# Working from PSUM in a spectral front, and a routing laid out without small copies

## The chip, the cores and the metric

One core of one Trainium2 chip runs the whole program in one launch. The metric is device time in microseconds (us). Engines are named as in the profile: PE is TensorE's matmul, PEld its weight load, DVE is VectorE, ACT is ScalarE, POOL is GpSimd, SP issues most of the DMAs.

## The reference, cut to what matters

```python
# front: x is (8, 3072, 256); 24576 tokens in all
X = np.fft.rfft(x, axis=1)                       # Xr, Xi
Yr = Xr @ w_r - Xi @ w_i + b_r
Yi = Xr @ w_i + Xi @ w_r + b_i
Y* = sign(Y*) * max(abs(Y*) - 0.01, 0)           # shrinkage
y  = np.fft.irfft(Y, n=3072, axis=1)             # token rows
# routing: 8 experts, the best one for each token
logits = y @ w_gate;  e = argmax(logits);  gate = softmax(logits)[e]
# experts, each on its own tokens
out[mask] = gate * (relu(y[mask] @ w1[e]) @ w2[e])
# last: two products, multiplied, then w3 and w_out
result = ((out @ W1) * (out @ W2)) @ w3 @ w_out
```

## The kernel before

The program has three parts: the front (transform, linear layer, shrinkage, inverse transform, routing), the experts (windows of 512 or 256 rows of one expert) and a last part of dense products. Every float32 product is made as three fp32r products of a high and a low part (`mm3`, L98); the high part is an ACT copy, the low part a subtraction on DVE or POOL.

The front factors 3072 = 48 x 64 and has three stages that run interleaved. Stage a (`stage_a`, L195) works on 64 tiles t: it loads a piece of x, splits it (`dxh` by ACT, `dxl` by POOL from t = 11 on), transforms over one factor and stores to DRAM. Stage b (`stage_b`, L235) makes 96 steps n, each for a pair of values k of k1. `dft2` (L246) multiplies into a PSUM bank; X gets the high part of it (ACT, L258), the low part (DVE, L259), and, for the second half of the linear layer, the negated first half of both parts (DVE, L262, SBUF to SBUF). X has three buffers and `dft2` runs three k ahead of the linear layer. `linear` (L264) makes 24 matmuls a k pair into a bank `pl`; then DVE adds the bias from `pl` into an SBUF tile s (L283 or L285), clamps s into m (L286) and subtracts m from s (L287), ACT rounds s into sh (L288) and DVE makes the low part sl (L289). `inv1` (L292) consumes sh and sl one step later. Stage c (`stage_c`, L325) works on 64 tiles t: `inv2` (L337) makes the token rows y, `flip` (L344) transposes them through PE, ACT and DVE split them (yh, yl, L351 and L352), `logits` (L355) multiplies by the gate weights. Four tiles t, as four groups g, are accumulated in one PSUM bank, and after the fourth `route` (L398) runs once for their 1536 tokens: 16 times in all.

`route` transposes the logits on DVE (L404), finds the expert by small DVE operations on 128 partitions x 12 x 8 (L415 to L435), counts tokens ahead of each by four doubling steps of an addition and a copy (L430, L431); and `late` (L437), one tile t later, adds a matmul for the rows above, gets the row in `xs`, moves 12 blocks of 32 x 8 into the layout of y by small copies (L452), casts the row numbers (L454), and writes gate and token number behind each row of y (L458, L459). The 16 rows of indices are then scattered by 16 indirect DMAs from POOL (L388), at most six for each tile t in program order.

The queue of each engine is in order. A planner (`schedule_with_timeline_sim=True`) places the instructions on the queues by its own model of costs, from the order of the program, the free buffers and the eight PSUM banks (pool `ps`, one bank a tile). The stages are interleaved in program order by L936 to L954: eight tiles of a and c for 12 steps of b, c lagging 15 steps.

Of the kernel before, what the change touches and what calls it, by code (L numbers as in the profile page):

```python
# [81 lines left out]
def misc_constants():  # L82
    ident = np.eye(128, dtype=np.float32)
    tri = np.zeros((128, 256), np.float32)
    tri[:, :128] = np.triu(np.ones((128, 128)), 1)
    tri[:, 128:] = 1.0
    small = np.zeros((128, 128), np.float32)
    small[:, 0:8] = 8 - np.arange(8)
    small[:, 8:16] = np.arange(8) * CAP
    small[:, 16:18] = np.where(np.arange(128) < 64, 1.0, -1.0)[:, None]  # L90
    small[96, 17] = 1.0
    small[:, 18:26] = np.arange(8)
    small[:, 32:96] = np.arange(64)
    small[:P96, 96:128] = np.arange(S).reshape(P96, 32)
    return [ident, tri, small]


def mm3(nc, out, a, b, first=True, last=True):  # L98
    """out (+)= a.T @ b, a and b as (high, low) parts; the product of the low parts is below float32's last bit."""
    nc.tensor.matmul(out, a[0], b[0], start=first, stop=False)  # L100
    nc.tensor.matmul(out, a[0], b[1], start=False, stop=False)  # L101
    nc.tensor.matmul(out, a[1], b[0], start=False, stop=last)  # L102


class Front:
# [17 lines left out]
    def const(self, pool, name, shape, src=None, fill=True):  # L123
        """A constant as (high, low) parts."""
# [39 lines left out]
    def consts_c(self, pool):  # L164
        nc = self.nc
        self.g2 = self.const(pool, "c_g2", [P96, P96])
        # gate weights, spread so that four quads of tokens land on four groups of partitions
        raw = self.p["s"].tile([128, 512], F32, name="s")
        wg = raw[:, :2 * NE].rearrange("p (c e) -> p c e", c=2)
        nc.sync.dma_start(wg, self.ins["moe_w_gate"].rearrange("(c p) e -> p c e", p=128))  # L170
        self.sg = pool.tile([128, 2, 4, 128], F32R, name="sg")
        nc.gpsimd.memset(self.sg.bitcast(F32), 0.0)
        for g in range(4):
# [3 lines left out]
        raw = self.p["s"].tile([128, 512], F32, name="s")  # L177
# [4 lines left out]
        zero = self.p["s"].tile([128, 2 * D], F32, name="s")  # L182
# [52 lines left out]
    def stage_b(self):  # L235
        """A step for each pair of values of k1, over all batches."""
# [9 lines left out]
        def dft2(n):  # L246
# [13 lines left out]
            if k:  # L260
                # [Q | P] is followed by -Q
                nc.vector.tensor_scalar(X[:, :, :, 128:192], X[:, :, :, 0:64].bitcast(F32), -1.0, None, op0=ALU.mult)  # L262

        def linear(n):  # L264
# [12 lines left out]
            s = self.p["s"].tile([128, 512], F32, name="s")  # L277
# [3 lines left out]
            if i:  # L281
                bias = self.bias[:, D:2 * D].unsqueeze(1).to_broadcast([128, 2, D])
                nc.vector.tensor_tensor(s.rearrange("p (k e) -> p k e", k=2), pl.rearrange("p (k e) -> p k e", k=2), bias, op=ALU.add)  # L283
# [41 lines left out]
    def stage_c(self):  # L325
# [18 lines left out]
        def flip(t):  # L344
            for c in range(2):
# [3 lines left out]
                yh = self.p["yt"].tile([128, 384], F32R, name="yh")  # L349
                yl = self.p["yt"].tile([128, 384], F32R, name="yl")  # L350
                nc.scalar.activation(out=yh, in_=pt[:, :384], func=AF.Copy)  # L351
                nc.vector.tensor_tensor(yl, pt[:, :384], yh.bitcast(F32), op=ALU.subtract)  # L352
                yt[t, c] = yh, yl

        def logits(t):  # L355
            g = t % 4
# [6 lines left out]
            if g == 3:  # L363
# [5 lines left out]
        for t in range(n + 3):  # L369
# [4 lines left out]
            if t < n:  # L374
                inv2(t)
            if 1 <= t < n + 1:
                flip(t - 1)
            late, self.late = self.late, None
            if 2 <= t < n + 2:
                logits(t - 2)  # L380
# [17 lines left out]
    def route(self, b, h, pg, ys):  # L398
        """Expert, gate and row of 1536 tokens: (g, t) x (jj, pb) has p = 32 pb + t, j = 8 g + 4 h + jj."""
        nc, r = self.nc, self.p["r"]  # L400
        V = nc.vector
        NC = 12
        lgt = r.tile([128, 384], F32, name="lgt")
        V.transpose(lgt, pg[:, :384])  # L404
        lg4 = lgt.rearrange("p (k i) -> p k i", i=32)

        def t3(name, dt=F32):
            return r.tile([128, NC, NE], dt, name=name)

        def wide(ap):  # L410
            return ap.to_broadcast([128, NC, NE])

        lg, sh, v, oh, ex = t3("lg"), t3("shf"), t3("vv"), t3("oh", BF16), t3("ex")
        m1 = [r.tile([128, NC, 1], F32, name=f"m1{i}") for i in range(4)]
# [3 lines left out]
        io = wide(self.small[:, 0:8].unsqueeze(1))  # L418
# [4 lines left out]
        pair = r.tile([128, NC, 2], F32, name="pair")  # L423
        # how many tokens of the same expert come before: in the columns before, and in the rows above
        W = NC * NE
        cur = oh.rearrange("p k e -> p (k e)")
        for i, d in enumerate((1, 2, 4, 8)):
            nxt = r.tile([128, W], BF16, name=f"pre{i}")
            n = d * NE
            V.tensor_tensor(nxt[:, n:], cur[:, n:], cur[:, :W - n], op=ALU.add)  # L430
            V.tensor_copy(nxt[:, :n], cur[:, :n])  # L431
            cur = nxt
        V.tensor_reduce(out=m1[2], in_=ex, axis=AX.X, op=ALU.add)
        V.tensor_scalar(m1[3], m1[2], 1e-9, None, op0=ALU.add)
        V.reciprocal(pair[:, :, 1:2], m1[3])  # L435

        def late():  # L437
            pr = self.ps.tile([128, 512], F32, name="ps")
            nc.tensor.matmul(pr[:, :W], self.tri[:, 0:128], oh.rearrange("p k e -> p (k e)"), start=True, stop=False)
            nc.tensor.matmul(pr[:, NE:W], self.tri[:, 128:256], cur[:, :W - NE], start=False, stop=True)  # L440
            nc.tensor.matmul(pr[:, 256:256 + NE], self.tri[:, 128:256], cur[:, W - NE:W], start=True, stop=True)
            rk, rs = t3("rk"), t3("rs")
            V.tensor_tensor(rk, pr[:, :W].rearrange("p (k e) -> p k e", e=NE), wide(self.cnt.unsqueeze(1)), op=ALU.add)
            V.tensor_tensor(rs, rk, oh, op=ALU.mult)
            V.tensor_reduce(out=pair[:, :, 0:1], in_=rs, axis=AX.X, op=ALU.add)
            V.tensor_tensor(self.cnt, self.cnt, pr[:, 256:256 + NE], op=ALU.add)
            # (g, t) x (jj, pb) -> (pb, t) x (g, jj)
            p2 = r.tile([P96, 4, 4, 2], F32, name="pair2")
            pv = pair.rearrange("p (k b) w -> p k b w", b=3)
            for g in range(4):  # L450
                for pb in range(3):
                    V.tensor_copy(p2[32 * pb:32 * pb + 32, g], pv[32 * g:32 * g + 32, :, pb, :])  # L452
            it = r.tile([P96, 16], I32, name="it", bufs=2)
            V.tensor_copy(it, p2[:, :, :, 0].rearrange("p g j -> p (g j)"))  # L454
            for g in range(4):
                # a row of xs: the row of y, its gate, its number
                j0 = 96 + 8 * g + 4 * h
                V.tensor_copy(ys[g][:, :, D], p2[:, g, :, 1])  # L458
                V.tensor_scalar(ys[g][:, :, D + 1], self.small[:P96, j0:j0 + 4], float(S * b), None, op0=ALU.add)  # L459
# [12 lines left out]
# Order of the last steps: b and c are stages of the front part, d is a step of the experts;  # L472
# the second string starts once the pools of the first stages are free.
# [3 lines left out]
class Experts:  # L477
    """The experts, over windows of rows of one expert each: 41 of 512 rows, and 21 of 256 rows.

    Whatever the counts, at least 41 full windows exist, and what they leave (3584 rows, in 8 parts) fits  # L480
    into 21 windows of 256: a part of n * 256 + r rows takes n + 1, of which the last one overlaps. Five
    batches and a half hold 26 full windows. The results are columns of dout, without gaps: first the experts of 256
    rows and more, then the others, in the order of their windows, as each of these spills over what the next
    one writes; the windows that are left over write behind the last column.
    """
# [13 lines left out]
    # small arithmetic on the counts  # L499
# [24 lines left out]
    def running(self, a, p=1):  # L524
        """Sums over the experts up to each, with it and without it."""
# [11 lines left out]
    def pick(self, w, incl, excl):  # L537
        """[1, w, 8]: whether window number w is one of the expert's."""
# [6 lines left out]
    def total(self, m, v, sh, out):  # L545
        """out = sum over the experts of m * v."""
# [6 lines left out]
    def full(self, w0, w1):  # L553
        """Windows w0 to w1 of 512 rows: the counts so far hold that many."""
# [26 lines left out]
    def rest(self):  # L581
        """The windows of 256 rows, and where every window's results go."""
# [18 lines left out]
        # the first column of every expert, against its first row of xs  # L601
# [425 lines left out]
```

## Time and profile before

| quantity | value |
|---|---|
| device time, three runs | 3786.15, 3791.05, 3792.51 us (median 3791.05) |
| span of the profiled execution | 3780.3 us (its time outside the span is not listed) |
| mean granted TensorE clock | 0.974 of full |
| busy over the span: PE, DVE, ACT, POOL | 95%, 53%, 45%, 36% |
| instructions: PE, DVE, ACT, POOL | 20592, 3595, 3073, 947 |

The share of busy time is a mean over parts with different limits. The front takes about the first 980 us; the experts come in from about 850 us; the last part begins at about 2100 us, and from there PE is busy without a gap. A matmul's duration in the trace is a latency: matmuls overlap, so the spacing of two starts is what one costs, and a PE that is busy all the time may still be short of its rate.

### The profile page before, as it was taken

The numbers are of one execution on the slowest core, as the hardware profiler recorded it, in microseconds if no ns is written. First come the engines' busy times: TensorE is split into PE (matmuls) and PEld (weight loads), VectorE is DVE, ScalarE is ACT, GpSimd is POOL, SyncE is SP. The second block draws the span as 40 slices with busy tenths as digits, with TensorE's granted clock in tenths as the row PEclk, the third lists the DMA queues.
The fourth block names the chain that finished last, engine by engine and source line by source line (L and its number), as shares of the span: only waits on it lengthen the run. The fifth ranks groups of instructions, "written<-read, shape, count | busy, mean of one in ns | idle before, by whom it ended". The sixth has DMA issues, their size and how long they took to land.

```text
span 3780.3 us, 56635 instructions
## 1 busy us (share of the span) xinstructions
PE 3599.0 (95%) x20592; PEld 3120.0 (83%) x20592; DVE 1995.8 (53%) x3595; ACT 1717.8 (45%) x3073; POOL 1357.6 (36%) x947
## 2 busy tenths in 40 slices
PE   7998888989899999999999999999999999999998
PEld 5987777877678888788888888888888888888887
DVE  5788888887755555455565333333333333333332
ACT  5665555546344555454545433333333333333333
POOL 4456566555644555555555211110111101111011
PEclk8999999988999999999999999999999999999999
DMA  8756565455565666566666401111011110111000
GB/s 236 228 173 176 161 174 169 139 152 156 155 161 140 172 176 163 155 168 166 173 161 162 115 27 34 34 33 30 29 34 34 31 30 30 34 34 31 26 23 17
DMA packets 335896, 410.82 MB, mean 109 GB/s; under 512 B 185728, under 2 KB 243200, under 8 KB 335616
## 3 DMA queue, kind: packets, MB, share of 16 engines
q1 hardware_dynamic: 314112, 356.65, 34.5%
q0 software_dynamic: 21504, 50.56, 4.2%
q8 instruction: 161, 2.64, 0.3%
q14 instruction: 119, 0.97, 0.1%
HBM read 277.12 MB, written 130.19 MB: 108 GB/s over the span
## 4 chain that ended last, share of the span: by engine, by line
PE 64%; DVE 17%; DMA 8%; issue 4%; ACT 3%; POOL 2%; SPq 1%; DVEq 0%; POOLq 0%; ACTq 0%
PE ps L101 21%; PE ps L102 21%; PE ps L100 21%; DMA bits<-in_w 4%; DVE X L262 3%; DMA raw<-in_wexp 2%; POOL xs L388 1%; DVE pair L452 1%; DVE hlo L685 1%; DVE dxl L657 1%; DMA xs<-y,it 1%; PE ps L255 1%; DVE s L287 1%; DVE m L286 1%; POOL wlo L673 1%
## 5 line engine op out<-in xcount | busy, mean ns | idle before, releaser
L673 POOL TENSOR_TENSOR wlo<-raw,whi 128x1024 fp32r<-128x1024 f32 x236 | 580.3, 2464 | 433.4 <-ACT whi L672 418.1
L874 POOL DMA_INDIRECT out_dram<-eo,eidx x192 | 184.1, 959 | 1466.5 <-ACT eo L873 1364.4
L685 DVE SCALAR_TENSOR_TENSOR hlo<-ps,hhi 128x512 fp32r<-128x512 f32 (+1 forms) x496 | 289.6, 594 | 405.0 <-ACT hhi L684 402.5
L863 ACT ACTIVATE ephi<-ep 128x512 fp32r<-128x512 f32 x384 | 241.6, 629 | 516.4 <-DVE ep L860 516.4
L860 DVE TENSOR_TENSOR ep<-ps,ea 128x512 f32<-128x512 f32 x384 | 265.7, 692 | 366.3 <-PE ps L102 361.9
L100 PE MATMUL ps<-mph,ephi 128*128 128x256 f32 x1536 | 432.5, 283 | 0.0
L101 PE MATMUL ps<-mpl,ephi 128*128 128x256 f32 x1536 | 432.5, 283 | 0.0
L102 PE MATMUL ps<-mph,eplo 128*128 128x256 f32 x1536 | 426.6, 283 | 0.0
L101 PE MATMUL ps<-hlo,whi 128*128 128x512 f32 (+1 forms) x992 | 356.5, 364 | 43.7 <-DVE hlo L685 43.5
L864 DVE TENSOR_TENSOR eplo<-ep,ephi 128x512 fp32r<-128x512 f32 x384 | 265.0, 690 | 228.8 <-ACT ephi L863 228.8
L684 ACT ACTIVATE hhi<-ps 128x512 fp32r<-128x512 f32 (+1 forms) x496 | 252.2, 520 | 272.9 <-PE ps L102 264.8
L100 PE MATMUL ps<-dxh,whi 128*128 128x512 f32 (+1 forms) x992 | 355.3, 358 | 0.8 <-ACT y L342 0.4
L101 PE MATMUL ps<-dxl,whi 128*128 128x512 f32 (+1 forms) x992 | 354.6, 357 | 0.0
L672 ACT ACTIVATE whi<-raw 128x1024 fp32r<-128x1024 f32 x248 | 262.2, 1058 | 203.1 <-DMA raw<-in_wexp 143.8
L102 PE MATMUL ps<-dxh,wlo 128*128 128x512 f32 (+1 forms) x992 | 354.3, 357 | 0.0
L102 PE MATMUL ps<-hhi,wlo 128*128 128x512 f32 (+1 forms) x992 | 352.5, 359 | 0.0
L101 PE MATMUL ps<-exl,m1h 128*128 128x512 f32 x768 | 303.9, 396 | 0.0
L100 PE MATMUL ps<-exh,m1h 128*128 128x512 f32 x768 | 303.9, 396 | 0.0
L100 PE MATMUL ps<-exh,m0h 128*128 128x512 f32 x768 | 303.8, 396 | 0.0
L102 PE MATMUL ps<-exh,m1l 128*128 128x512 f32 x768 | 303.8, 396 | 0.0
L102 PE MATMUL ps<-exh,m0l 128*128 128x512 f32 x768 | 303.7, 395 | 0.0
L101 PE MATMUL ps<-exl,m0h 128*128 128x512 f32 x768 | 303.7, 395 | 0.0
(197 smaller groups left out, 8635.7 us busy)
## 6 DMA issues: line engine op xcount, KB each, us to landing
raw<-in_wexp SPq DMA_DIRECT2D x248, 512.0 KB, 5.2
dx<-in_x SPq DMA_DIRECT2D x64, 384.0 KB, 4.0
zs<-raw SPq DMA_DIRECT2D x64, 384.0 KB, 3.5
z<-zs SPq DMA_DIRECT2D x192, 128.0 KB, 3.8
vs<-v SPq DMA_DIRECT2D x192, 128.0 KB, 3.0
vq<-vs SPq DMA_DIRECT2D x64, 384.0 KB, 4.0
ex<-dout SPq DMA_DIRECT2D x48, 512.0 KB, 3.5
dx<-xs SPq DMA_DIRECT2D x164, 128.0 KB, 2.6
```

The source lines that it names most:

```text
L100: nc.tensor.matmul(out, a[0], b[0], start=first, stop=False)
L101: nc.tensor.matmul(out, a[0], b[1], start=False, stop=False)
L102: nc.tensor.matmul(out, a[1], b[0], start=False, stop=last)
L262: nc.vector.tensor_scalar(X[:, :, :, 128:192], X[:, :, :, 0:64].bitcast(F32), -1.0, None, op0=ALU.mult)
L672: nc.scalar.activation(out=hi, in_=raw, func=AF.Copy)
L673: (nc.gpsimd if s >= 12 else nc.vector).tensor_tensor(lo, raw, hi.bitcast(F32), op=ALU.subtract)
L684: nc.scalar.activation(out=hi[:, :T], in_=ph[:, :T], func=AF.Relu)
L685: nc.vector.scalar_tensor_tensor(out=lo[:, :T], in0=ph[:, :T], scalar=0.0, in1=hi[:, :T].bitcast(F32), op0=ALU.max, op1=ALU.subtract)
L860: nc.vector.tensor_tensor(p, ps[1], a, op=ALU.mult)
L863: nc.scalar.activation(out=hi, in_=p, func=AF.Copy)
L864: nc.vector.tensor_tensor(lo, p, hi.bitcast(F32), op=ALU.subtract)
L874: ins = nc.gpsimd.indirect_dma_start(out=self.out, out_offset=bass.IndirectOffsetOnAxis(ap=idx[:, n:n + 1], axis=0), in_=o[:, n, :], in_of ...
```

## The change

Four things are edited. (1) The negated half of X is made from the PSUM bank: its high part by an ACT copy with scale -1, its low part by DVE as high minus PSUM. (2) The bias sum, the clamp's input and the shrunk value stay in the bank `pl`; the SBUF tiles s, and their pool, are gone. (3) `logits` takes two tiles t at once: for each of three blocks pb of 32 rows it multiplies the 32-wide pieces of that block, gathered by a strided moving operand of 8 x 32 columns, into 96 output rows; two such groups share a bank. So p = 32 pb + t of the logits is already p of y; `route` works on 96 partitions x 16 x 8. (4) The 12 block copies, the cast, the writes behind y and the copies beside the doubling additions go: the additions read zeros ahead of five standing tiles `pre`, the last reduction writes int32, and gate and number are put behind y by ACT (one activation for the numbers, four copies). The 1e-9 is added from a table by a tensor_tensor. `logits` stands ahead of `flip` in the program order.

```diff
     # dft2
             if k:
-                nc.vector.tensor_scalar(X[:, :, :, 128:192], X[:, :, :, 0:64].bitcast(F32), -1.0, None, op0=ALU.mult)
+                nc.scalar.activation(out=X[:, 0, :, 128:192], in_=src[:, :, 0:64], func=AF.Copy, scale=-1.0)
+                nc.vector.tensor_tensor(X[:, 1, :, 128:192], X[:, 0, :, 0:64].bitcast(F32), src[:, :, 0:64], op=ALU.subtract)
     # linear
-                nc.vector.tensor_tensor(s, pl, self.bias[:, :2 * D], op=ALU.add)
-            nc.vector.tensor_scalar(m, s, LAM, -LAM, op0=ALU.min, op1=ALU.max)
-            nc.vector.tensor_tensor(s, s, m, op=ALU.subtract)
-            nc.scalar.activation(out=sh, in_=s, func=AF.Copy)
-            nc.vector.tensor_tensor(sl, s, sh.bitcast(F32), op=ALU.subtract)
+                nc.vector.tensor_tensor(pl, pl, self.bias[:, :2 * D], op=ALU.add)
+            nc.vector.tensor_scalar(m, pl, LAM, -LAM, op0=ALU.min, op1=ALU.max)
+            nc.vector.tensor_tensor(pl, pl, m, op=ALU.subtract)
+            nc.scalar.activation(out=sh, in_=pl, func=AF.Copy)
+            nc.vector.tensor_tensor(sl, pl, sh.bitcast(F32), op=ALU.subtract)
     # logits
-            for c in range(2):
-                yh, yl = yt.pop((t, c))
-                nc.tensor.matmul(lg[0][:, :384], self.sg[:, c, g], yh, start=g == 0 and c == 0, stop=False)
-                nc.tensor.matmul(lg[0][:, :384], self.sg[:, c, g], yl, start=False, stop=g == 3 and c == 1)
+            out = lg[0][:P96, 256 * g:256 * g + 256].rearrange("p (k t) -> p k t", t=32)
+            steps = [(c, w, pb) for c in range(2) for w in range(2) for pb in range(3)]
+            for c, w, pb in steps:
+                mv = yt[u, c][w].rearrange("p g (j b t) -> p (g j) b t", b=3, t=32)[:, :, pb]
+                nc.tensor.matmul(out, self.sg[:, c, pb], mv, start=(c, w, pb) == steps[0], stop=(c, w, pb) == steps[-1])
     # route
-            V.tensor_tensor(nxt[:, n:], cur[:, n:], cur[:, :W - n], op=ALU.add)
-            V.tensor_copy(nxt[:, :n], cur[:, :n])
+            V.tensor_tensor(pre[i + 1][:, 8:], pre[i][:, 8:], pre[i][:, 8 - d:8 + NC - d], op=ALU.add)
-        V.tensor_scalar(m1[3], m1[2], 1e-9, None, op0=ALU.add)
+        V.tensor_tensor(m1[3], m1[2], self.small[:P96, 26:27].unsqueeze(1).to_broadcast([P96, NC, 1]), op=ALU.add)
     # late
-            V.tensor_reduce(out=pair[:, :, 0:1], in_=rs, axis=AX.X, op=ALU.add)
+                V.tensor_reduce(out=it.unsqueeze(2), in_=rs, axis=AX.X, op=ALU.add)
-                    V.tensor_copy(p2[32 * pb:32 * pb + 32, g], pv[32 * g:32 * g + 32, :, pb, :])
-            V.tensor_copy(it, p2[:, :, :, 0].rearrange("p g j -> p (g j)"))
-                V.tensor_copy(ys[g][:, :, D], p2[:, g, :, 1])
-                V.tensor_scalar(ys[g][:, :, D + 1], self.small[:P96, j0:j0 + 4], float(S * b), None, op0=ALU.add)
+            nc.scalar.activation(out=mt[:, :, 1].rearrange("p (g j) -> p g j", g=4), in_=num, func=AF.Copy, bias=float(S * b))
+                nc.scalar.activation(out=ys[g][:, :, D:RW], in_=mt[:, 4 * g:4 * g + 4], func=AF.Copy)
     # build
-        front.pools(ctx_ab, z=2, X=3, X0=1, s=2)
+        front.pools(ctx_ab, z=2, X=3, X0=1)
```

## Rows read from the trace of the kernel before

**Rows 1.** Windows from route to route: span, busy (instructions) by engine, clock, DMA, GB/s

```profile
216.00:271.00 55.00, 46.52 (x332) 41.42 (x331) 47.61 (x101) 31.08 (x67) 35.40 (x32) 0.96 0.63 180
...
608.00:664.00 56.00, 47.99 (x335) 42.98 (x334) 47.63 (x100) 31.03 (x67) 35.46 (x32) 0.94 0.57 163
664.00:715.00 51.00, 46.52 (x328) 41.86 (x327) 42.09 (x99) 27.27 (x59) 28.31 (x27) 0.93 0.50 148
...
761.00:804.00 43.00, 41.85 (x316) 39.08 (x315) 40.33 (x126) 21.93 (x47) 26.36 (x24) 0.96 0.48 136
```

**Rows 2.** Timeline, DVE: start, length, engine, line, operation, tiles, shapes

```profile
480.92 9.20 DVE L262 TENSOR_SCALAR X<-X 128x256 fp32r<-128x256 f32 x1
```

**Rows 3.** Timeline, POOL, around the same time; the last column is idle before

```profile
479.13 0.92 POOL L388 DMA_INDIRECT xs<-y,it  x1 [0.30 <-issue]
480.07 2.54 POOL L232 TENSOR_TENSOR vl<-vq,vh 96x512 fp32r<-96x512 f32 x2
...
487.50 2.47 POOL L208 TENSOR_TENSOR dxl<-dx,dxh 96x512 fp32r<-96x512 f32 x2
```

**Rows 4.** Timeline, PE, around the same time

```profile
484.81 0.28 PE L101 MATMUL ps<-w_r_l,X 128*128 128x256 f32 x1
484.92 0.28 PE L102 MATMUL ps<-w_r_h,X 128*128 128x256 f32 x1
490.18 0.58 PE L100 MATMUL ps<-w_i_h,X 128*128 128x256 f32 x1 [4.98 <-DVE X L262]
```

**Rows 5.** Line L262 alone: duration ns min/median/max, first and last start

```profile
L262 DVE TENSOR_SCALAR X<-X x184: 272/287/10653, 54.7 to 826.8; 128x256 fp32r<-128x256 f32 x184
```

**Rows 6.** Windows of 25 us, one before the first scatter and one with a stall

```profile
175.00:200.00 25.00, 25.00 (x186) 23.09 (x185) 16.97 (x32) 18.25 (x39) 11.47 (x10) 1.00 0.59 175
...
475.00:500.00 25.00, 20.02 (x133) 18.27 (x132) 20.83 (x25) 11.58 (x26) 16.63 (x14) 0.86 0.47 142
```

**Rows 7.** Groups by line, 216 to 1000 us, DVE: busy us, mean ns, idle before

```profile
L262 DVE TENSOR_SCALAR X<-X 128x256 fp32r<-128x256 f32 x133 | 122.4, 920 | 1.5
...
L259 DVE TENSOR_TENSOR X<-ps,X 128x256 fp32r<-128x256 f32 x133 | 55.3, 416 | 28.5 <-ACT X L258 26.5 <-ACT dxh L207 1.6
L289 DVE TENSOR_TENSOR sl<-s,sh 128x512 fp32r<-128x512 f32 x71 | 55.2, 777 | 23.7 <-ACT sh L288 23.2
L287 DVE TENSOR_TENSOR s<-s,m 128x512 f32<-128x512 f32 x71 | 51.9, 731 | 0.4 <-DVE y L459 0.2
L452 DVE COPY pair<-pair 32x8 f32<-32x8 f32 x192 | 47.9, 249 | 3.4
L286 DVE TENSOR_SCALAR m<-s 128x512 f32<-128x512 f32 x70 | 46.5, 665 | 1.5
L283 DVE TENSOR_TENSOR s<-ps,bias 128x512 f32<-128x512 f32 x65 | 44.0, 677 | 1.0 <-PE ps L102 0.9
...
L417 DVE TENSOR_TENSOR shf<-lg,m 128x96 f32<-128x96 f32 x16 | 11.0, 686 | 0.5
```

**Rows 8.** Groups by line, 216 to 664 us, ACT

```profile
L258 ACT ACTIVATE X<-ps 128x256 fp32r<-128x256 f32 x92 | 32.4, 383 | 21.6 <-PE ps L255 21.4
...
L422 ACT ACTIVATE ex<-shf 128x96 f32<-128x96 f32 x8 | 2.3, 284 | 4.7 <-DVE shf L417 4.7
```

**Rows 9.** Waits of PE up to 1050 us: in total, times, longest us

```profile
PE ps L361 <- DVE s L283: 8.4, 6, 2.5
```

**Rows 10.** Timeline, PE: logits matmuls back to back

```profile
506.01 0.34 PE L361 MATMUL ps<-yh,sg 128*128 128x384 f32 x1
506.19 0.34 PE L362 MATMUL ps<-yl,sg 128*128 128x384 f32 x1
```

**Rows 11.** Groups by line, 216 to 664 us, POOL

```profile
L388 POOL DMA_INDIRECT xs<-y,it x128 | 122.0, 953 | 48.9 <-issue 30.2 <-DVE y L458 12.3 <-DMA xs<-y,it 1.8
L232 POOL TENSOR_TENSOR vl<-vq,vh 96x512 fp32r<-96x512 f32 x64 | 83.4, 1323 | 58.5 <-ACT vh L231 58.4
```

**Rows 12.** Chain of waits, 200 to 800 us: start, us, what

```profile
752.67 5.95 DVE sl L289
```

More of the change, by code (lines that the diff above doesn't have):

```diff
@@ L92, in misc_constants @@
     small[:, 18:26] = np.arange(8)
+    small[:, 26] = 1e-9
     small[:, 32:96] = np.arange(64)
@@ L166, in consts_c @@
         self.g2 = self.const(pool, "c_g2", [P96, P96])
-        raw = self.p["s"].tile([128, 512], F32, name="s")
+        raw = self.p["m"].tile([128, 512], F32, name="m")
         wg = raw[:, :2 * NE].rearrange("p (c e) -> p c e", c=2)
         nc.sync.dma_start(wg, self.ins["moe_w_gate"].rearrange("(c p) e -> p c e", p=128))
-        self.sg = pool.tile([128, 2, 4, 128], F32R, name="sg")
+        self.sg = pool.tile([128, 2, 3, P96], F32R, name="sg")
         nc.gpsimd.memset(self.sg.bitcast(F32), 0.0)
-        for g in range(4):
+        for g in range(3):
             hi = self.sg[:, :, g, 32 * g:32 * g + 8]
@@ L181, in consts_c @@
         nc.vector.tensor_copy(self.cnt, self.small[:, 8:16])
-        zero = self.p["s"].tile([128, 2 * D], F32, name="s")
+        self.pre = [pool.tile([P96, 64 + 128], BF16, name=f"pre{i}") for i in range(5)]
+        for t in self.pre:
+            nc.gpsimd.memset(t[:, :64], 0.0)
+        zero = self.p["m"].tile([128, 2 * D], F32, name="m")
         nc.gpsimd.memset(zero, 0.0)
@@ L348, in flip, with logits @@
                     nc.tensor.transpose(pt[:, 96 * j:96 * j + 96], ys[t][:, j, 128 * c:128 * c + 128], self.ident[:P96, :P96])
[L349 to L350 removed]
+                if t % 2 == 0:
+                    yt[t // 2, c] = [self.p["yt"].tile([128, 2, 384], F32R, name=n) for n in ("yh", "yl")]
+                yh, yl = [v[:, t % 2] for v in yt[t // 2, c]]
                 nc.scalar.activation(out=yh, in_=pt[:, :384], func=AF.Copy)
                 nc.vector.tensor_tensor(yl, pt[:, :384], yh.bitcast(F32), op=ALU.subtract)
[L353 to L356 removed]
+        def logits(u):
+            g = u % 2
             if g == 0:
                 lg[0] = self.ps.tile([128, 512], F32, name="ps")
+            out = lg[0][:P96, 256 * g:256 * g + 256].rearrange("p (k t) -> p k t", t=32)
[3 more added lines that the diff above has]
+                nc.tensor.matmul(out, self.sg[:, c, pb], mv, start=(c, w, pb) == steps[0], stop=(c, w, pb) == steps[-1])
             for c in range(2):
[L360 to L363 removed]
+                yt.pop((u, c))
+            if g:
+                t = 2 * u + 1
                 self.late = self.route(t // 8, t % 8 // 4, lg[0], [ys.pop(i) for i in range(t - 3, t + 1)])
@@ L375, in stage_c @@
                 inv2(t)
+            late, self.late = self.late, None
+            if t % 2 and t > 2:
+                logits((t - 3) // 2)
             if 1 <= t < n + 1:
                 flip(t - 1)
-            late, self.late = self.late, None
-            if 2 <= t < n + 2:
-                logits(t - 2)
             if late:
@@ L401, in route, with t3 @@
         V = nc.vector
-        NC = 12
-        lgt = r.tile([128, 384], F32, name="lgt")
-        V.transpose(lgt, pg[:, :384])
+        NC = 16
+        lgt = r.tile([P96, 512], F32, name="lgt")
+        V.transpose(lgt, pg[:P96])
         lg4 = lgt.rearrange("p (k i) -> p k i", i=32)
-        def t3(name, dt=F32):
-            return r.tile([128, NC, NE], dt, name=name)
+        pre = [t.rearrange("p (k e) -> p k e", e=NE) for t in self.pre]
+        def t3(name):
+            return r.tile([P96, NC, NE], F32, name=name)
         def wide(ap):
-            return ap.to_broadcast([128, NC, NE])
-        lg, sh, v, oh, ex = t3("lg"), t3("shf"), t3("vv"), t3("oh", BF16), t3("ex")
-        m1 = [r.tile([128, NC, 1], F32, name=f"m1{i}") for i in range(4)]
+            return ap.to_broadcast([P96, NC, NE])
+        lg, sh, v, ex = t3("lg"), t3("shf"), t3("vv"), t3("ex")
+        oh = pre[0][:, 8:]
+        m1 = [r.tile([P96, NC, 1], F32, name=f"m1{i}") for i in range(4)]
         V.tensor_tensor(lg, lg4[:, :, 0:8], lg4[:, :, 8:16], op=ALU.add)
@@ L417, in route @@
         V.tensor_tensor(sh, lg, wide(m1[0]), op=ALU.subtract)
-        io = wide(self.small[:, 0:8].unsqueeze(1))
+        io = wide(self.small[:P96, 0:8].unsqueeze(1))
         V.scalar_tensor_tensor(out=v, in0=sh, scalar=0.0, in1=io, op0=ALU.is_equal, op1=ALU.mult)
@@ L433, in route @@
+        mt = r.tile([P96, NC, 2], F32, name="mt")
         V.tensor_reduce(out=m1[2], in_=ex, axis=AX.X, op=ALU.add)
-        V.tensor_scalar(m1[3], m1[2], 1e-9, None, op0=ALU.add)
-        V.reciprocal(pair[:, :, 1:2], m1[3])
+        V.tensor_tensor(m1[3], m1[2], self.small[:P96, 26:27].unsqueeze(1).to_broadcast([P96, NC, 1]), op=ALU.add)
+        V.reciprocal(mt[:, :, 0:1], m1[3])
         def late():
             pr = self.ps.tile([128, 512], F32, name="ps")
[L439 to L443, printed above, removed]
-            V.tensor_tensor(rs, rk, oh, op=ALU.mult)
-            V.tensor_reduce(out=pair[:, :, 0:1], in_=rs, axis=AX.X, op=ALU.add)
-            V.tensor_tensor(self.cnt, self.cnt, pr[:, 256:256 + NE], op=ALU.add)
-            p2 = r.tile([P96, 4, 4, 2], F32, name="pair2")
-            pv = pair.rearrange("p (k b) w -> p k b w", b=3)
-            for g in range(4):
-                for pb in range(3):
-                    V.tensor_copy(p2[32 * pb:32 * pb + 32, g], pv[32 * g:32 * g + 32, :, pb, :])
-            it = r.tile([P96, 16], I32, name="it", bufs=2)
-            V.tensor_copy(it, p2[:, :, :, 0].rearrange("p g j -> p (g j)"))
-            for g in range(4):
-                j0 = 96 + 8 * g + 4 * h
-                V.tensor_copy(ys[g][:, :, D], p2[:, g, :, 1])
-                V.tensor_scalar(ys[g][:, :, D + 1], self.small[:P96, j0:j0 + 4], float(S * b), None, op0=ALU.add)
@@ new lines, in late @@
+            up, all_ = self.tri[:P96, 0:P96], self.tri[:P96, 128:128 + P96]
+            first, last = self.pre[0], self.pre[4]
+            nc.tensor.matmul(pr[:P96, :W], up, first[:, 64:], start=True, stop=False)
+            nc.tensor.matmul(pr[:P96, NE:W], all_, last[:, 64:64 + W - NE], start=False, stop=True)
+            nc.tensor.matmul(pr[:P96, 256:256 + NE], all_, last[:, 64 + W - NE:], start=True, stop=True)
+            rk, rs = t3("vv"), t3("lg")
+            V.tensor_tensor(rk, pr[:P96, :W].rearrange("p (k e) -> p k e", e=NE), wide(self.cnt[:P96].unsqueeze(1)), op=ALU.add)
@@ new lines, in late @@
+            V.tensor_tensor(rs, rk, oh, op=ALU.mult)
+            it = r.tile([P96, NC], I32, name="it", bufs=2)
+            with nc.allow_low_precision(reason="whole numbers below 2^18, one of each eight is not zero"):
+                V.tensor_reduce(out=it.unsqueeze(2), in_=rs, axis=AX.X, op=ALU.add)
+            V.tensor_tensor(self.cnt[:P96], self.cnt[:P96], pr[:P96, 256:256 + NE], op=ALU.add)
+            num = self.small[:P96, 96:128].rearrange("p (g h j) -> p g h j", g=4, h=2)[:, :, h]
```

11 lines of the change are left out of this document (3 added, 8 removed).

## Prediction

> **What bounds the kernel now.** I read the table by windows first. Cut from route to route, the front repeats: eight periods from 216 to 664 us take 448 us, 56 each, then three shorter ones (140 us to 804) once stage a has run out [rows 1]. In each of the eight DVE is busy for some 47.6 us, PE for 48, POOL for 35.5, ACT for 31: two engines look nearly full at once. The reader is to see what hides in both.
>
> The timeline of DVE shows one negation of X (L262) that takes 9.20 us [rows 2]; the median of this line is 0.287 us, its longest 10.65 [rows 5]. POOL has just ended its sixteenth scatter and runs eight splits back to back, from 480.07 to 489.97 [rows 3]; the negation starts among them and ends 0.15 us behind the last. So DVE's operation does not run for 9 us: it waits for POOL's row of splits. PE meanwhile runs dry: 4.98 us idle in front of the matmul that needs the negated half [rows 4], and then comes back at half rate: the 25 us window around it has a granted clock of 0.86, that is, part of it at 1.2 instead of 2.4 GHz [rows 6]. I find such a stall once per period.
>
> Two numbers tell what a period would be without it. PE: before the first scatter it is busy 25.00 of 25 us with 186 matmuls at full clock [rows 6], 0.134 us each, so the 335 matmuls of a period need 45.0 us. From the other side: 56 us less the 4.98 of idleness [rows 4] and less 3.4 us lost at half clock (1 - 0.94 of 56 [rows 1]) leaves 47.6. The last part of the span, from 2100 us on, and the experts before it, are touched by nothing here: what the front gives up is given to the total.
>
> **The change part by part.**
>
> *Negated X.* 184 operations on DVE, SBUF to SBUF, go. Their mean from 216 us on is 0.920 against the median of 0.287 [rows 5, 7]: 133 x 0.633 = 84 us of pure waiting in 133 of them. In their place stand 184 subtractions of 128 elements with one operand in PSUM. The nearest row is L259, same operand places, 256 elements, 0.416 us, and it shows nothing of the stalls [rows 7]; half the elements cost less, so I put 0.29, no change against the uncontended median (bounds 0.208, half of that row, and 0.416: -15 to +24 us of DVE time). ACT gets 184 copies of 128 elements: between 0.284 and 0.383 us [rows 8], so about 0.33 x 11.5 = 3.8 us a period.
>
> Here the Trainium skill has a rule: by "SBUF — State Buffer", section "Who interferes with whom", a tensor_scalar between SBUF operands can take the port pair that DVE shares with GpSimd, one of the two waits for the whole instruction of the other, and an operation with a PSUM operand stays out of it. The trace agrees with the first half (9.20 us). The same section says that two SBUF inputs contend with GpSimd's reads as well; that speaks against part of the gain and is the first rival below.
>
> *Shrinkage in PSUM.* Five operations a step stay five. Bias sum: 0.677 us as before, its output now in PSUM, which no row shows; I take 0.677 (bounds 0.665 and 0.777, L286 and L289 [rows 7]: -1 to +10 us of DVE over 96 steps). The clamp reads PSUM: I take L283's 0.677 against its mean of 0.665 now. The subtraction goes from 0.731 and the low part from 0.777 to 0.677, as both lose their second SBUF input [rows 7]: 96 x 0.15 = 14 us of DVE less. None of it is on the path by itself while DVE has room; if it had none, it would be worth 14 us.
>
> The bank `pl` is now held through five operations instead of one, at least 4 x 0.65 = 2.6 us longer, 96 times: 250 bank-us of the 8 x 772 that stage b has [rows 5]. Waits of PE for a bank behind L283 exist but are small, 8.4 us in 6 places [rows 9]. The logits bank is held for two pairs instead of four tiles, which gives some back. I put 0; bounds -8 and, if every second step waited the 1.4 us of these places, +67.
>
> *Logits.* 16 matmuls of 384 columns a period, 0.18 us apart [rows 10], are 2.9 us. 24 of 256 columns, 0.11 apart as in the linear layer [rows 4], are 2.6. The moving operand is strided in runs of 32, which no row shows: I put 0, bounds -0.3 and, at double spacing, +2.6 us a period, 42 us in 16.
>
> *Routing.* 192 block copies of 0.249 us go, 47.9 us [rows 7], 3.0 a period, and with them the copies beside the additions, the cast and the writes behind y; wider rows (128 elements for 96) and five small ACT operations (at most 0.284 each [rows 8], 1.4 us a period) come. DVE then needs 47.6 - 8.9 (stall) - 3.0 - 0.9 = 34.8 us a period, ACT 31 + 3.8 + 1.4 = 36. Neither is the bound. The scatters need their indices: the chain in front of them gets some 5 us shorter, which counts once, behind the last route.
>
> *What is late next.* PE with 45.0 us, POOL with 35.5 us busy and 30.2 / 8 = 3.8 us of issue gaps between scatters [rows 1, 11], 39.2 together, none of which the change touches. POOL's splits behind the scatters are due about when the shorter period wants them. I therefore do not give the full 11 us: 46.5 us a period, between 45.0 and 47.6.
>
> **Sum.** 8 x (56 - 46.5) = 76. The three periods to 804 us need, at 322 matmuls each (mean of the first and the last [rows 1]) and 0.134 us, 43.3; I take 44.3, so 140 - 133 = 7. Behind that 5 for the last route. Together 88 us: the span goes from 3780.3 to 3692. The median of the three runs is 10.8 us above that span, which I add unchanged: **3703 us**. With 42 us a period (linear matmuls at their 0.11 us, not the mean pace) 8 x 14 + 15 + 10 = 137 us would go, 3654; with 49 us, 8 x 7 = 56, 3735. That is the own range of this case.
>
> **The rivals.**
>
> *The lock stays with the routing.* Its additions and comparisons keep two SBUF inputs, and some run while POOL catches up. For it: a subtraction with two SBUF inputs, L289, took 5.95 us [rows 12], and L417, 96 elements, has a mean of 0.686 us [rows 7]. Against it: it is one operation of a route and not of every step, and it must meet the 10 us of splits. A stall of 5.95 instead of 9.20 us costs 6.1 of the 9.5 now lost, so 8 x 3.4 + 7 = 34 us are left: 3757.
>
> *PSUM is short.* The longer hold of `pl` makes every second step wait 1.4 us: 3703 + 67 = 3770. For it: the waits of [rows 9]. Against it: they are few while DVE is stalled.
>
> *Slower: X waits in a zigzag.* The negated parts are made by ACT and then DVE, in the bank that DVE reads for the low part. If the bank is handed from ACT to DVE to ACT to DVE, each k step gets ACT's turn into its chain: two instructions ahead of it in ACT's queue, 0.28 and 0.38 us [rows 8], and its own 0.28, 0.94 together, behind which stand the copies for the inverse transform. Place: PE in front of the second half of the linear layer, 184 times. Price in full: 173 us, 3876. It decides from 88 / 184 = 0.48 us of wait per k step. Against it: X is made three k ahead, a quarter of a period's 12 or some 11 us, and DVE no longer blocks.
>
> By the skill's "PSUM — Partial Sum Buffer", section "PSUM bank collisions raise a hardware error", two engines may not touch a bank at once even to read, which asks for this zigzag. No row here shows ACT and DVE reading one bank without a dependence.
>
> *It does not do what it says.* The next SBUF operation inherits the wait, or the planner lays the queues so that PE waits elsewhere: 3791.
>
> **Chances.** The forecast 0.60; lock in the routing 0.17; PSUM 0.08; zigzag 0.09; no effect 0.06. The range 3655 to 3772 leaves out the zigzag, no effect and some 0.04 of the forecast below it. A measurement can tell 0.2% (7.6 us): faster 0.84, same 0.06, slower 0.10.
>
> **What would show it.** L262's successor on DVE without any duration above 1 us, the clamp too; periods of 45 to 48 us with PE's clock near 1.00; POOL's splits still eight in a row and DVE working through them. Wrong if a routing addition shows 5 to 10 us, if PE waits for ACT or DVE behind the negated copy, if logits matmuls stand more than 0.15 us apart, or if the periods shrink and the experts give it back.

## The result, and the profile after

The changed kernel takes 3690.77 us (median of 4 runs, 3681.56 to 3694.26) beside 3791.78 for the kernel before (3786.15 to 3797.92) on the same chip: a ratio of 0.973 with a 95% interval of 0.9714 to 0.9747, some 101 us less. This holds for the chip on which it was taken; on another one the experiments below found no gain, and on a further one kernels close to it gained 0.2% at most.

The profiled execution has a span of 3679.8 us, 100.5 less than before. Its page, busy time by engine (share of the span, instructions):

```profile
PE 3551.0 (97%) x20720; PEld 3089.0 (84%) x20720; DVE 1835.4 (50%) x3193; ACT 1762.4 (48%) x3337; POOL 1342.6 (36%) x952
```

The windows from route to route answer to [rows 1], with the same columns (span, busy and instructions of PE, PEld, DVE, ACT, POOL, granted clock, DMA share, GB/s):

```profile
228.50:275.20 46.70, 46.25 (x349) 41.95 (x348) 34.82 (x77) 34.77 (x85) 35.29 (x33) 1.00 0.70 205
...
455.40:500.50 45.10, 44.63 (x338) 40.66 (x337) 33.64 (x73) 33.60 (x83) 34.92 (x33) 1.00 0.66 193
...
591.50:633.80 42.30, 41.38 (x318) 38.22 (x317) 33.17 (x75) 28.86 (x73) 27.50 (x26) 1.00 0.59 169
633.80:674.50 40.70, 40.70 (x332) 38.89 (x332) 31.90 (x74) 26.35 (x67) 25.36 (x25) 1.00 0.61 171
674.50:711.10 36.60, 35.78 (x289) 33.95 (x288) 33.75 (x99) 23.74 (x63) 21.83 (x22) 1.00 0.58 161
```

The reader sees one engine full where there were two: PE is busy for 44.63 of 45.10 us at a clock of 1.00, and DVE, ACT and POOL each have some 10 us of air. Along the span the difference lies so, cut at the route transposes (215.9 to 663.6 to 938.6 us before, 228.5 to 591.5 to 840.4 after):

| stretch | before | after | change |
|---|---|---|---|
| up to the first route | 215.9 | 228.5 | +12.6 |
| eight periods | 447.7 | 363.0 | -84.7 |
| the seven shorter ones behind | 275.0 | 248.9 | -26.1 |
| behind the last route | 2841.7 | 2839.4 | -2.3 |

The new DVE operation of the negation, all 184 of it (duration in ns min/median/max, first and last start, forms), and the clamp, which now reads PSUM, answer to [rows 5]:

```profile
L268 DVE TENSOR_TENSOR X<-X,ps x184: 219/277/291, 57.3 to 732.3; 128x128 fp32r<-128x128 f32 x184
L292 DVE TENSOR_SCALAR m<-ps x96: 669/680/691, 62.5 to 739.5; 128x512 f32<-128x512 f32 x96
```

POOL still has a row of splits behind its last scatter, as in [rows 3], here five pairs from 490.32 to 502.84 us:

```profile
489.38 0.92 POOL L399 DMA_INDIRECT xs<-y,it  x1 [0.30 <-issue]
490.32 2.52 POOL L237 TENSOR_TENSOR vl<-vq,vh 96x512 fp32r<-96x512 f32 x2
...
500.31 2.53 POOL L237 TENSOR_TENSOR vl<-vq,vh 96x512 fp32r<-96x512 f32 x2
```

No DVE operation of a step waits for that row any more: the longest negation is 0.291 us where it was 10.65, the longest clamp 0.691.

What stands against the gain is in one place. The DVE timeline before the first route has a hole, and PE's waits up to 1000 us (in total, times, longest) begin with its consequence:

```profile
95.57 0.69 DVE L292 TENSOR_SCALAR m<-ps 128x512 f32<-128x512 f32 x1 [11.36 <-DMA xs<-m]
```

```profile
PE ps L101 <- ACT sh L294: 19.7, 5, 16.3
```

The zero tile behind `xs` comes from pool `m`, which has one buffer, instead of pool `s` with two. SP's sixteen stores of zeros read it; the next clamp, L292, wants that buffer, and DVE stands for 11.36 us. In the window from 75 to 100 us PE issues 61 matmuls; the kernel before issues 151 there.

### The profile page after: what moved, and what is told of

The parts are those of the page before. It is cut to its first block, busy times and chain, and to the rows that moved or that the text cites. A ratio compares the mean times of both kernels' runs of the same rounds, so it can differ in the third digit from the quotient of the medians.

```text
span 3679.8 us, 56676 instructions
## 1 busy us (share of the span) xinstructions
PE 3551.0 (97%) x20720; PEld 3089.0 (84%) x20720; DVE 1835.4 (50%) x3193; ACT 1762.4 (48%) x3337; POOL 1342.6 (36%) x952
## 4 chain that ended last, share of the span: by engine, by line
PE 73%; DVE 9%; DMA 7%; issue 4%; POOL 2%; ACT 1%; SPq 1%; POOLq 0%; DVEq 0%; ACTq 0%
PE ps L102 23%; PE ps L103 23%; PE ps L101 23%; DMA bits<-in_w 4%; PE ps L260 2%; DMA raw<-in_wexp 2%; PE ps L370 1%; DVE hlo L689 1%; DVE dxl L661 1%; POOL wlo L677 1%; DVE cva L792 1%; DVE cva L791 1%; PE ps L354 1%; POOL xs L399 1%; DVE pre L439 0%
```

## The experiments

The first four kernels ran on one chip, where the kernel before takes 3789.84 us. The record doesn't name the chip of the result above; its kernel before is within 2 us of this one, and I take both for one, the first chip. These four take the edits apart.

**Edit 1 alone: the negated halves from PSUM, in the kernel before.**

```
- nc.vector.tensor_scalar(X[:, :, :, 128:192], X[:, :, :, 0:64].bitcast(F32), -1.0, None, op0=ALU.mult)
+ nc.scalar.activation(out=X[:, 0, :, 128:192], in_=src[:, :, 0:64], func=AF.Copy, scale=-1.0)
+ nc.vector.tensor_tensor(X[:, 1, :, 128:192], X[:, 0, :, 0:64].bitcast(F32), src[:, :, 0:64], op=ALU.subtract)
```

> The kernel before with the negated halves of X alone made from PSUM (ACT copy, DVE subtraction); shrinkage and routing as before. Theory (a lock: any DVE operation between SBUF operands in the fast mode waits for POOL's row of splits, and the next such operation inherits the wait): the clamp, SBUF to SBUF, stands in every step and takes the stall over; the time stays within 25 us of before, 3765 to 3795, and the clamp L287 shows durations of 5 to 10 us. Rival (the gain is DVE work and waiting taken out, edit by edit): 84 us of waiting in L262 go, some 60 us of the time, 3730, and no line of DVE inherits 9 us.

Measured: 3782.90 us, ratio 0.9982 (0.9972 to 0.9992). The DVE timeline in one period, and POOL's beside it (start, length, engine, line):

```profile
478.19 0.28 DVE L263 TENSOR_TENSOR X<-X,ps 128x128 fp32r<-128x128 f32 x1
478.38 9.57 DVE L287 TENSOR_SCALAR m<-s 128x512 f32<-128x512 f32 x1
```

```profile
477.77 2.54 POOL L232 TENSOR_TENSOR vl<-vq,vh 96x512 fp32r<-96x512 f32 x2
...
485.19 2.47 POOL L208 TENSOR_TENSOR dxl<-dx,dxh 96x512 fp32r<-96x512 f32 x2
```

The stall has moved. The clamp, one SBUF input and SBUF output, now starts in POOL's row and ends 0.29 us behind it (487.95 against 487.66). The negation itself shows none (0.290 us is its longest), and yet the period is 55.0 us (217.5 to 657.7 in eight). Moving one of the operations that wait is worth 7 us.

Seven of the eight periods have the stall on the clamp. In the eighth it is on the subtraction behind it, L288, which has two SBUF inputs; it begins 0.55 us before POOL's row and ends 0.56 us behind it (379.07 against 378.51), which is about its own length:

```profile
368.11 10.96 DVE L288 TENSOR_TENSOR s<-s,m 128x512 f32<-128x512 f32 x1
```

```profile
368.66 2.53 POOL L232 TENSOR_TENSOR vl<-vq,vh 96x512 fp32r<-96x512 f32 x2
...
376.04 2.47 POOL L208 TENSOR_TENSOR dxl<-dx,dxh 96x512 fp32r<-96x512 f32 x2
```

**Edit 2 alone: the shrinkage in PSUM, in the kernel before.**

```
- nc.vector.tensor_tensor(s, pl, self.bias[:, :2 * D], op=ALU.add)
- nc.vector.tensor_scalar(m, s, LAM, -LAM, op0=ALU.min, op1=ALU.max)
- nc.vector.tensor_tensor(s, s, m, op=ALU.subtract)
+ nc.vector.tensor_tensor(pl, pl, self.bias[:, :2 * D], op=ALU.add)
+ nc.vector.tensor_scalar(m, pl, LAM, -LAM, op0=ALU.min, op1=ALU.max)
+ nc.vector.tensor_tensor(pl, pl, m, op=ALU.subtract)
...
```

> The kernel before with the bias sum, the clamp and the shrunk value alone kept in PSUM; negation and routing as before. Theory (lock): the negation stays SBUF to SBUF and keeps the stalls; 3775 to 3800. Rival (edit by edit): some 14 us of DVE work and 18 us of waiting in the clamp go, 3765.

Measured: 3769.27 us, ratio 0.9948 (0.9932 to 0.9965), 6 us below what the lock alone gives and nearer to the rival. I read this as DVE's saved time counting for something while DVE is still short of time; no run shows that by itself. The negation keeps its stall, one of 9.6 to 10.5 us in each period, and the period is 54.5 us:

```profile
L262 DVE TENSOR_SCALAR X<-X x184: 270/283/10481, 60.8 to 808.2; 128x256 fp32r<-128x256 f32 x184
```

**Both, with the old routing.** The two diffs above together.

> Both edits of stage b, the routing as before. Theory (lock): no fast-mode SBUF operation is left in the steps, only the small copies of the routing; these can still meet the splits, once per route. Most of the gain comes: 3700 to 3735, more than the sum of the two edits alone; periods of 45 to 49 us. Rival (edit by edit): the sum of the two single edits, whatever they measure.

Measured: 3730.16 us, ratio 0.985 (0.9834 to 0.9867): 60 us less, where the two alone come to 7 + 21 = 28. The edits are not a sum: as long as one DVE operation between SBUF tiles is left in each step, it takes the stall. What waits now is a write of 4 elements a row in the routing, which the change also takes away:

```profile
318.46 4.29 DVE L460 TENSOR_SCALAR y<-t_small 96x4 f32<-96x4 f32 x1
```

```profile
320.23 2.48 POOL L232 TENSOR_TENSOR vl<-vq,vh 96x512 fp32r<-96x512 f32 x2
```

It ends at 322.75, POOL's last split at 322.71. Such a wait stands in each of eight periods (3.75 to 4.78 us); the period is 49.7.

**The change with the old negation.** The diff of edit 1 reversed in the changed kernel.

> The changed kernel with the old negation (tensor_scalar, SBUF to SBUF) put back; shrinkage and routing as changed. Theory (lock): one operation per k in the fast mode is enough to bring the stalls back: L267 with durations up to 9 us, periods over 52 us, 3760 to 3790. Rival (edit by edit): the routing's and the clamp's share of the gain stays, 3730 or less.

Measured: 3749.21 us, ratio 0.9893 (0.9876 to 0.9910), between the two expectations, which both missed; the period is 51.3. The negation waits twice in each period, once for the single pair of splits between the scatters and once for the row. It meets the row 3.5 to 4 us behind its start, so the second wait is some 6.3 us here and not 9:

```profile
311.06 2.43 DVE L267 TENSOR_SCALAR X<-X 128x256 fp32r<-128x256 f32 x1
...
319.36 6.35 DVE L267 TENSOR_SCALAR X<-X 128x256 fp32r<-128x256 f32 x1
```

So in company the new negation is worth 101 - 41 = 60 us and the routing with its logits 101 - 60 = 41 us, and 7 us is what the negation is worth alone.

The next four kernels ran on a second chip, where the kernel before takes 3871.71 us, and the last four on a third, where it takes 3892.07. Their totals can't be set beside those above, as the changed kernel without a further edit on the third chip shows, so it stands first.

**The changed kernel again.** No edit.

> The changed kernel, nothing edited, as the yardstick of the next three. If the gain lies in DVE's waits behind POOL and nothing else, it is what it was: ratio 0.973, some 3690 us, with first route at 228 us and periods of 45. If what showed in the last runs (waits in the front that the trace gives no releaser for, periods of 58 us) comes with the chip and not with the edits, then on that chip this kernel too has such periods and stands at 0.998 to 1.000 of the kernel before.

Measured on the third chip: 3894.95 us against 3892.07, ratio 1.0006 (0.9995 to 1.0018). The gain is not there. The first two windows are of this run (same columns as above), the two behind of the changed kernel on the first chip:

```profile
100.00:200.00 100.00, 99.53 (x741) 92.85 (x741) 63.97 (x135) 71.94 (x169) 41.24 (x33) 0.98 0.74 209
300.00:400.00 100.00, 81.82 (x529) 72.20 (x528) 50.09 (x111) 54.26 (x134) 62.61 (x59) 0.85 0.49 143
```

```profile
100.00:200.00 100.00, 99.28 (x746) 92.71 (x746) 63.60 (x136) 71.59 (x168) 41.98 (x33) 0.99 0.75 210
300.00:400.00 100.00, 99.05 (x744) 89.85 (x743) 71.78 (x158) 74.99 (x181) 78.32 (x73) 1.00 0.72 208
```

Up to the first scatter the two chips go alike (741 and 746 matmuls); with scatters the third does 529 where the first does 744, and its eight periods are 59.7 us each. DVE shows no lock there: its negation is never above 0.3 us. The timelines inside a stretch with scatters show the place, first the third chip (PE, SP, ACT, then PE again), then the first of these matmuls, SP's load and ACT's copy on the first chip:

```profile
425.36 0.61 PE L260 MATMUL ps<-d,z 128*128 128x128 f32 x4
...
427.18 0.60 PE L260 MATMUL ps<-d,z 128*128 128x256 f32 x2
...
431.17 2.06 SPq L249 DMA_DIRECT2D z<-zs  x4
431.18 0.38 ACT L263 ACTIVATE X<-ps 128x256 fp32r<-128x256 f32 x1 [5.44 <-remote]
...
432.10 0.58 PE L101 MATMUL ps<-sh,c_g_h 128*128 128x256 f32 x1 [3.86 <-issue]
```

```profile
381.88 0.61 PE L260 MATMUL ps<-d,z 128*128 128x128 f32 x4
...
382.52 1.76 SPq L249 DMA_DIRECT2D z<-zs  x4
382.53 0.38 ACT L263 ACTIVATE X<-ps 128x256 fp32r<-128x256 f32 x1 [0.27 <-PE ps L260]
```

ACT's copy of X and SP's load of z both wait for PE's matmuls L260. On the first chip they start within 0.04 us of their end (381.88 + 0.61). On the third they start together at 431.17, though the same four matmuls ended at 425.97 and the last L260 in front of them at 427.78. PE tells the others that a matmul is done by a step of a counter, a semaphore, and the trace records these steps. I take for each of PE's steps from 200 to 1000 us the first record behind the end of its matmul: on the first chip none of 1107 comes over 0.35 us late, here 133 of 972 come over 1 us late, the latest by 16.1 (73 of the program's 3265 steps have no record here, so these lags are upper bounds). On the second chip the kernel with all splits on DVE, below, has 168 of 883. What holds the steps back I can't tell from this, nor whether the kernel before has such lags there: it was not traced on these two chips.

**Zeros in a tile of their own.**

```
- zero = self.p["m"].tile([128, 2 * D], F32, name="m")
+ zero = self.p["X0"].tile([128, 2, 2, 256], F32R, name="X0").rearrange("p h c w -> p (h c w)")[:, :RW].bitcast(F32)
```

> The changed kernel, with the zeros that clear the rows of xs in the free tile of X0 instead of the single buffer m. Theory: the hole of 11.4 us on DVE and 16.3 us on PE near 84 us is the clamp's wait for the 16 stores of zeros that leave from m; it goes, and the front ends 11 to 16 us earlier: 3674 to 3680, against some 3689 of the changed kernel. Rival: the hole is the load of the pipeline itself (PE has to wait for X or the first transforms anyway); within 5 us of the changed kernel.

> The changed kernel with its zeros in a tile of their own, so that no clamp waits for the sixteen stores of zeros. If that wait is the 12.6 us by which the first route came later, the route moves from 228 to about 217 us and the whole takes 8 to 13 us less than the changed kernel beside it. Rival, that PE is short of other inputs there and finds another wait: 0 to 4 us less.

Measured: 3863.47 us on the second chip (ratio to before 0.9983, 0.9969 to 0.9997); on the third 3889.48 (0.9992, 0.9983 to 1.0001), 5.5 us below the changed kernel beside it, with intervals that overlap. The local reading is firm, as the scatters have not begun: DVE's hole is gone, in the window from 75 to 100 us PE issues 100 matmuls in place of 57, and the first route comes at 223.8 instead of 229.2. That is 5.4 us, less than half of the 12.6 that I had expected: the stores are the cause of that part.

```profile
75.00:100.00 25.00, 16.36 (x100) 14.62 (x101) 14.60 (x35) 12.83 (x30) 7.48 (x6) 0.80 0.59 170
```

For the rest the traces show a place, but no run tests it. With the zeros gone, DVE waits at about the same time for another of the three constants that now come from the single buffer `m`, the gate weights:

```profile
84.34 2.12 DVE L176 CAST sg<-m 128x16 fp32r<-128x16 f32 x3 [4.77 <-DMA m<-in_moe_w_gate]
```

The first routes on the first chip point there too: 217.5 with edit 1, 215.4 with edit 2 and 219.8 with both, so the larger part of the way from 215.9 to 228.5 comes with the rest of the diff, which moves the constants among other things.

**The negation with two SBUF inputs.** In the changed kernel, -2 x + x:

```
+ x = X[:, :, :, 0:64].bitcast(F32)
+ nc.vector.scalar_tensor_tensor(out=X[:, :, :, 128:192], in0=x, scalar=-2.0, in1=x, op0=ALU.mult, op1=ALU.add)
```

> The changed kernel with the negation as one scalar_tensor_tensor (-2 X + X) with both inputs in SBUF, which has no fast mode. Theory A (two SBUF inputs wait for POOL's splits too): durations of 2 to 6.5 us on this line behind the scatters, as with the old negation, 3745 to 3765. Theory B (only the fast mode waits): every one takes some 0.41 us, DVE has 1.6 us a period more than in the changed kernel, 3685 to 3700.

> The changed kernel with one DVE operation for the negation again, in a form with two SBUF inputs (-2 x + x) in place of the one-input form of the kernel before. If only the one-input form between SBUF operands waits for POOL, no stall of over 2.5 us, and at most 15 us more than the changed kernel: 3685 to 3705. If two SBUF inputs wait as well, as long as the one-input form did when it was put back: 3745 to 3765.

Measured: 3870.53 us on the second chip (1.0006, 0.9990 to 1.0023) and 3896.70 on the third (1.0013, 1.0004 to 1.0023). The totals tell nothing there, the durations do (second chip, then third):

```profile
L268 DVE SCALAR_TENSOR_TENSOR X<-X x184: 350/415/2136, 54.1 to 873.6; 128x256 fp32r<-128x256 f32 x184
```

```profile
L268 DVE SCALAR_TENSOR_TENSOR X<-X x184: 353/415/1520, 53.7 to 886.5; 128x256 fp32r<-128x256 f32 x184
```

Two SBUF inputs wait too, here for one or two splits (one is some 1.26 us). Whether they would wait for a whole row these two runs can't tell, for there is none to meet: from 100 to 860 us POOL's back-to-back splits stand in pairs (94 and 91 of them), with two rows of four and one, and none of eight. The first chip has the answer. The subtraction L288 of edit 1 alone waited for a whole row of eight (10.96 us), and in the kernel before L289 took 5.93 us at 752.67 [rows 12], behind a row of four. So these traces show no difference between one SBUF input and two.

**Less work for PE.** The zeros apart, and the low parts of y left out of the logits, which halves their matmuls; the routing then rests on rounded logits.

```
- steps = [(c, w, pb) for c in range(2) for w in range(2) for pb in range(3)]
+ steps = [(c, w, pb) for c in range(2) for w in range(1) for pb in range(3)]
```

> The kernel of y1 with the low parts of y left out of the logits, so the routing is a little different from the reference: 192 matmuls of 256 columns less, 0.12 us each, 23 us of PE, nothing else changed. Theory (PE is now the bound of the periods): 14 to 22 us less than y1, periods of 43.5 to 44 us. Rival (POOL or DVE sets the 45.1 us): within 5 us of y1, periods unchanged.

> The kernel with the zeros apart, which also leaves out the low parts of y in the logits: 12 matmuls of 256 columns in place of 24 per pair of steps, some 192 of 384 in all that are no longer there. If PE is the bound of the front now, at 0.12 us each that is 23 us, less what PE waits elsewhere: 14 to 22 us less than the kernel with the zeros apart. If POOL's scatters and splits or DVE set the period, 0 to 5 us less.

Measured: 3872.23 us on the second chip (1.0005, 0.9992 to 1.0019) and 3891.78 on the third (1.0002, 0.9993 to 1.0011): 8.8 and 2.3 us more than the kernel with the zeros apart, so no gain. So PE is not the bound of the front on these chips once scatters run; before them the first route comes earlier by 2.6 us (221.2 for 223.8 on the third). That it is on the first rests on the windows alone; this run did not get to test it there.

**All splits on DVE,** in the kernel before, so that POOL has only scatters.

```
- (nc.gpsimd if i == 0 or t > 10 else nc.vector).tensor_tensor(l, src, h.bitcast(F32), op=ALU.subtract)
+ nc.vector.tensor_tensor(l, src, h.bitcast(F32), op=ALU.subtract)
...
- parts[t, i] = self.split(vq[:, 512 * i:512 * (i + 1)], "v", "vector" if b == B - 1 else "gpsimd")
+ parts[t, i] = self.split(vq[:, 512 * i:512 * (i + 1)], "v", "vector")
```

> The kernel before with the low parts of x and of the inverse transform's input all made on DVE instead of POOL; POOL keeps only the scatters, DVE gets some 11 us a period more. Theory (the splits hold the lock, the scatters do not): no DVE operation of the steps above 2 us, DVE 49 us a period without stalls, periods of 50 to 52 us, 3735 to 3760. Rival (the scatters hold it too): stalls of 5 us and more remain, and with DVE fuller the time is 3790 or more.

Measured on the second chip: 3820.99 us, ratio 0.9874 (0.9848 to 0.9899). The old negation, untouched, beside 256 scatters but none of the front's splits on POOL:

```profile
L262 DVE TENSOR_SCALAR X<-X x184: 224/283/424, 55.7 to 831.9; 128x256 fp32r<-128x256 f32 x184
```

```profile
L287 DVE TENSOR_TENSOR s<-s,m 128x512 f32<-128x512 f32 x73 | 49.8, 682 | 0.2
```

Its longest is 0.424 us where it was 10.65 [rows 5], and the subtraction with two SBUF inputs, L287, has a mean of 0.682 from 200 to 1000 us where it had 0.731 [rows 7]. 31 of its negations run beside a scatter, and the longest of these is the 0.424 us; without one the longest is 0.30. So scatters alone hold DVE by no more than some 0.1 us; that the splits hold it is shown by the ends that fall together on the first chip, since the kernel before was not traced on this one. The periods are 55.9 us (216.0 to 663.1 in eight) and not the 50 to 52 expected, with DVE free of stalls. Why this kernel gains on a chip where variants of the change do not was not tried further.

## Why the prediction was right, point by point

The forecast was 3703 us, measured were 3690.77, inside the forecast's own range; the mechanism is the one it named.

- **The stall is a lock behind POOL's splits, and PE is behind it.** Shown: without splits no negation waits; with splits one of the DVE operations between SBUF tiles that are left waits until POOL's row ends, in four different lines: L262, L287 and L460 end within 0.3 us of it, L288 within 0.6. The prediction names the negation alone; in the kernel before one of the eight stalls is already on the clamp (L286, 9.58 us at 256.83). The Trainium skill's "SBUF — State Buffer", section "Who interferes with whom", has a DVE instruction with at most one SBUF input, outside the two-port modes, not contend with GpSimd; the trace agrees: 0.291 us is the longest of 184 (L268).
- **46.5 us a period.** It is 45.4 (363.0 / 8). I kept 1.5 us for POOL's splits coming late to PE; PE's waits for POOL from 200 to 860 us are 1.3 us for `vl` and 0.9 for `dxl`. The bound from PE was right: 338 matmuls in 45.1 us are 0.133 each, 0.134 were taken.
- **DVE 34.8 and ACT 36 a period.** 33.6 and 33.6 in the window from 455.4 us. The subtraction that takes the negation's place is 0.273 us where 0.29 was put, ACT's negated copy 0.275 where 0.33 was; shrinkage is 0.68 to 0.70 an operation where 0.677 was put.
- **The three shorter periods, -7.** They gave -20.7 (140.3 to 119.6). This term was mis-sized: I took 322 matmuls each at 0.134 us and a us on top. There are 318, 332 and 289, and at full clock they come to 0.127 each. Before, each of the three had a stall of its own (4.97, 5.93 and 4.77 us, on L262, L289 and L286), of which the prediction names the second alone, under a rival. What lies behind them gave 5.3 and 2.3, for which 5 stood.
- **Up to the first route, 0.** The sum has no such term, and 12.6 us were lost. The diff moves three constants from pool `s` to pool `m`; I read it as a renaming and did not count the sixteen stores that hold the one buffer. A moved tile brings the DMAs that read it along.
- **Logits, 0.** Strided in runs of 32, the matmuls stand 0.12 us apart at 256 columns (three of 0.28 us each take 0.51 together):

```profile
497.17 0.51 PE L370 MATMUL ps<-yl,sg 128*96 128x256 f32 x3
```

- **The rivals.** The lock in the routing is there, in small for most routes: L428 with two SBUF inputs has a median of 0.698 and a longest of 1.748 us. That is a matter of where it falls: in six of the eight periods it starts 10.95 us into a row of some 12.5 and waits for the end alone. In the last route L454, also with two SBUF inputs, took 5.31 us behind splits of the experts (849.40). PSUM is not short: from 200 to 860 us PE's list of waits has one behind the shrinkage, 1.3 us for `sh`. The zigzag is real and costs next to nothing: ACT's negated copy waits for DVE's read of the same bank, PE's matmuls wait for X nowhere in their list up to 1000 us, and its weight loads wait 2.1 us for L268, in nine places. "No effect" is nearly what the single edits show (7 and 21 us), and what the third chip shows.

```profile
L428 DVE TENSOR_TENSOR lg<-lgt x16: 265/698/1748, 229.9 to 841.2; 96x128 f32<-96x128 f32 x16
```

```profile
ACT X L267 <- DVE X L264: 69.1, 114, 2.3
```

So 88 were forecast and 100.5 came: -85 for -76, -21 for -7, -8 for -5, and +12.6 for nothing. That the total came so close is in part luck: the loss that the sum lacks took back half of what the other terms gave beyond their forecast.

## What to carry to other kernels

Where a DVE operation of 0.3 us shows 9 us, look at POOL at the same time, and count every operation between SBUF tiles behind it, those with two SBUF inputs too: the next one inherits the stall, so the edits are worth little one by one (7 and 21 us) and much together (60, and 101 with the routing). When a diff moves a tile to another pool, count who holds that pool's buffers, DMAs too. And say on which chip a gain was measured: the same kernel took 2.7% off on one chip and nothing on another, where PE's steps were recorded late; whether the old wait stands there as well is not shown.

## What the runs showed of the hardware

A DVE operation between SBUF tiles that meets POOL's row of back-to-back splits can wait for the whole row and not for one split: 9.57 us for four pairs with one SBUF input, 10.96 us for four pairs with two. Not each one does; in pairs of splits many waited for one alone (1.38 us in the kernel before). Some of the long waits begin before the row's first record, while the last scatter is still recorded (at 366.90 us in the kernel before, the row at 367.54); the traces do not say why. Scatters without splits, 0.92 us each and 0.30 apart, hold DVE by no more than some 0.1 us. And of three chips, two run the kernel before in 82 and 102 us more than the first; on both, engines resume several us behind the step that should release them, in the kernel with all splits on DVE on the second and in the changed kernel on the third, and the stretches where I looked at this have scatters in them.
